# Attention and experts on one core: transposes with 112 columns, scores without their masked quarter, one two-bank PSUM tile

## The chip, the cores and the metric

The kernel runs on one core of one Trainium2 chip. The metric is the device time in microseconds, from the first to the last instruction of the program on that core. The times below are of repeated executions; the profile is one further execution under the hardware profiler.

## The reference

A gated linear attention with a state per head, and then a mixture of eight experts of which each token uses one:

```
B, H, S, D = 4, 8, 768, 48
for t in range(S):
    state = alpha[:, :, t, :, None] * state + einsum('bhd,bhe->bhde', k[:, :, t], v[:, :, t])
    y[:, :, t] = einsum('bhd,bhde->bhe', q[:, :, t], state)
x = y as [B * S, H * D]                     # 3072 tokens, 384 features
logits = x @ w_gate + modality_bias[modality_id]
e_idx = argmax(logits); gate_w = softmax(logits)[e_idx]
for e in range(8):                          # w1 384 x 1024, w2 1024 x 384
    mask = e_idx == e
    out[mask] = gate_w[mask] * (relu(x[mask] @ w1[e]) @ w2[e])
```

## The kernel before

**Attention.** The 768 positions of each of four batches are cut into chunks of P = 128, which makes NU = 24 chunks, NC = 6 to a batch. Heads go in NP = 4 pairs; a pair lies in 128 columns, its two heads at 0 to 47 and at 64 to 111, with fill between and behind (48 and 16 columns of which hold constants). For each chunk alpha, keys and queries are loaded as [position, pair of heads] and turned by TensorE with an identity matrix (`trans`, L242, four transposes to a tensor) into [feature, position]. ScalarE copies the turned alpha to X (L251). VectorE runs two scans over the chunk's positions, one backwards (G, L256) and one forwards (Fw, L266), and multiplies the turned keys by G (kh, L282) and the turned queries by Fw (qh, L290). After that a chunk needs matmuls only:

- `natural` (L296) turns kh back into [position, feature]; ScalarE copies it to knat (L298).
- `scores` (L308) forms, for each head, keys times queries, as [source position, query position], in 16 calls of K = 48, 64 sources and 128 queries. The first head of each pair goes to one one-bank PSUM tile and the second to another, both named sc, of a ring with two places. ScalarE copies each to SBUF (L312, scT), and GpSimd sets what lies above the diagonal to zero (L313, one mask of 128 x 512 for each tile).
- `state` (L328) multiplies the state T1 by qh, and `outputs` (L335) adds v times the masked scores, into y.
- `update` (L353) forms knat times v in kv; ScalarE copies it (L355), and GpSimd adds the old state (L357) and scales by the decay (L359), which gives the next T1.

**The order.** TensorE, VectorE and ScalarE issue in the order in which the program is written (their schedule is manual); GpSimd's and SyncE's instructions are placed by the framework's scheduler, which also works out all waits between engines. The loop `for s in range(NU)` is a software pipeline: step s turns and scans chunk s, scales chunk s - 1 (`scale`) and forms its scores and its update, finishes the outputs of chunk s - 2, and writes the rows of chunk s - 3 (`rows`, L366) to memory, from where tokens are gathered later. Routing (gate logits L378, choice of the expert, places in lists) is done in pieces between these, and small products of it use the PSUM name sc too. The order of TensorE in a step is: the transposes, `natural`, `logits`, `state(s - 2)`, `scores(s - 1)`, `outputs(s - 2)`, `update(s - 1)`.

**Experts.** Tokens of an expert are gathered (GpSimd's indirect DMA, xg, L689; their gate weights gg, L695), turned (L970) and split into a high and a low part (xH, xL), as are the weights (w1H, w1L, w2H, w2L). Each product is three matmuls. A slot's first layer (L1016 to L1018) writes to tiles tr; ScalarE and VectorE apply relu and split (hH L824, hL L826). The second layer takes the slot in units of 128 tokens: `layer2` makes 24 matmuls of 128x384 for a unit (L997 to L999), all into one PSUM tile op, taken as a place of the ring sc, and then `store` lets ScalarE scale it by the gate weights into SBUF (os, L1031), from where GpSimd's DMA scatters it to the output (L963). The slots come in this order: E0 and E1 with two units each (tokens known early), S1, S2 and S3 with four, S4 with four and, between its units, the steps of `short` (the short slot H of at most 32 tokens: L1055, L1067, L1074, beginning with transposes into a place of sc), S5 with four. The last unit of all is stored in another tile (of).

PSUM has the ring sc (two places of one bank), the ring tr (three), kv, and y.

## Time and profile before

| | us |
|---|---|
| median of 3 runs | 372.45 |
| lowest, highest | 371.29, 372.73 |
| the profiled execution, its time | 370.39 |
| its span in the profile | 368.4 |
| busy: TensorE | 356.4 (97%) |
| busy: VectorE | 219.1 (59%) |
| busy: ScalarE | 189.5 (51%) |
| busy: GpSimd | 154.5 (42%) |

About 2.0 us of the profiled execution lie around the span. Engines are named PE (TensorE's matmuls), PEld (its weight loads), DVE (VectorE), ACT (ScalarE), POOL (GpSimd) and SP (SyncE). In the time line a row gives the start, the duration, the engine, the line of the kernel, the operation, the tile written and those read, and the count of instructions run together in the row; behind it stands, in square brackets, how long the engine was idle before and what ended that. Rows of groups give, behind the bar, busy time, mean duration in ns, and the idle time of the engine ahead of them with what ended it. The mean granted clock of TensorE is 0.996. fp32 matmuls appear in the trace as two records to each call, transposes as one.

### The profile page before, as it was taken

To read this page: it belongs to the slowest core of one execution; us is meant where nothing else is said; L and a number is where in the kernel's file an instruction comes from. 1 tells how busy PE (TensorE), PEld (TensorE's weight loads), DVE (VectorE), ACT (ScalarE), POOL (GpSimd) and SP (SyncE) were. 2 spreads that over 40 slices of the span, in tenths; PEclk is the share of its full clock that TensorE was granted. 3 is DMA by queue.
4 is the path that set the end of the run, shared out by engine and by line. 5 is a ranking of instruction groups with operands and counts; after the bars stand their busy time and mean duration, and the time that the engine had idled before them with its cause. 6 is when DMAs were issued, how large, how long until landed. Compare 5 with 4: busy or idle time off the path is not lost. (4 is left out here: it accounts for less than half of the span.)

```text
span 368.4 us, 9336 instructions
## 1 busy us (share of the span) xinstructions
PE 356.4 (97%) x3666; PEld 315.6 (86%) x3666; DVE 219.1 (59%) x420; ACT 189.5 (51%) x367; POOL 154.5 (42%) x236
## 2 busy tenths in 40 slices
PE   8899999999999999999899999999999999999993
PEld 4689888889888887899788998899889988978992
DVE  6877979777979985888555415522660456036400
ACT  2766777777767764347454325524551554154310
POOL 9845346435436663047247326313712471220021
PEclk9999999999999999999999999999999999999998
DMA  9999999999999994887756317332733473110011
GB/s 135 166 161 178 187 190 206 195 181 189 200 198 184 213 347 165 292 323 240 246 149 220 107 62 254 111 107 83 240 93 122 133 226 134 44 44 5 1 45 50
DMA packets 122730, 59.18 MB, mean 161 GB/s; under 512 B 102857, under 2 KB 114168, under 8 KB 122676
## 3 DMA queue, kind: packets, MB, share of 16 engines
q1 hardware_dynamic: 118196, 48.78, 58.8%
q0 software_dynamic: 4032, 9.68, 7.7%
q8 instruction: 31, 0.51, 0.6%
q14 instruction: 23, 0.19, 0.2%
q10 hardware_dynamic: 448, 0.01, 0.1%
HBM read 49.01 MB, written 9.50 MB: 159 GB/s over the span
## 5 line engine op out<-in xcount | busy, mean ns | idle before, releaser
L963 POOL DMA_INDIRECT out_dram<-os,odx x23 | 23.5, 1023 | 102.9 <-ACT os L1031 93.2
L997 PE MATMUL sc<-w2H,hH 128*128 128x384 f32 x192 | 65.1, 339 | 0.0
L999 PE MATMUL sc<-w2H,hL 128*128 128x384 f32 x192 | 64.2, 334 | 0.0
L998 PE MATMUL sc<-w2L,hH 128*128 128x384 f32 x192 | 64.2, 334 | 0.0
L834 DVE TENSOR_TENSOR w1L<-w1r,w1H 128x768 fp32r<-128x768 f32 x24 | 22.0, 956 | 65.6 <-ACT w1H L832 65.6
L1016 PE MATMUL tr<-xH,w1H 128*128 128x512 f32 (+1 forms) x144 | 53.8, 374 | 0.0
L1018 PE MATMUL tr<-xH,w1L 128*128 128x512 f32 (+1 forms) x144 | 53.5, 372 | 0.0
L1017 PE MATMUL tr<-xL,w1H 128*128 128x512 f32 (+1 forms) x144 | 53.5, 371 | 0.0
L826 DVE SCALAR_TENSOR_TENSOR hL<-tr,hH 128x512 fp32r<-128x512 f32 x47 | 32.4, 689 | 30.6 <-ACT hH L824 30.6
L824 ACT ACTIVATE hH<-tr 128x512 fp32r<-128x512 f32 x47 | 28.1, 598 | 43.1 <-PE tr L1018 41.7
L1031 ACT ACTIVATE os<-sc,gg 128x384 f32<-128x384 f32 x23 | 13.4, 582 | 66.9 <-PE sc L999 40.7
L313 POOL TENSOR_SCALAR_AFFINE_SELECT scT<-scT 128x512 f32<-128x512 f32 x48 | 38.7, 830 | 21.6 <-ACT scT L312 21.5
L695 POOL DMA_INDIRECT gg<-gd,idx x25 | 27.0, 1079 | 27.5 <-DMA gd<-gs 20.5
L997 PEld LDWEIGHTS sc<-w2H,hH 128*128 128x128 f32 x192 | 36.1, 188 | 1.1 <-issue 1.0
L998 PEld LDWEIGHTS sc<-w2L,hH 128*128 128x128 f32 x192 | 36.1, 188 | 0.1
L999 PEld LDWEIGHTS sc<-w2H,hL 128*128 128x128 f32 x192 | 36.0, 188 | 0.0
L266 DVE TENSOR_TENSOR_SCAN Fw<-X,DF 128x516 f32<-128x516 f32 x24 | 32.4, 1351 | 0.8
L312 ACT COPY scT<-sc 128x512 f32<-128x512 f32 x48 | 25.8, 590 | 11.9 <-PE sc L308 11.5
L689 POOL DMA_INDIRECT xg<-xd,idx x25 | 26.5, 1059 | 11.5 <-issue 4.9
L1018 PEld LDWEIGHTS tr<-xH,w1L 128*128 128x128 f32 x144 | 27.1, 188 | 4.7
L1017 PEld LDWEIGHTS tr<-xL,w1H 128*128 128x128 f32 x144 | 27.1, 188 | 4.6
L1016 PEld LDWEIGHTS tr<-xH,w1H 128*128 128x128 f32 x144 | 27.1, 188 | 4.6
(244 smaller groups left out, 674.2 us busy)
## 6 DMA issues: line engine op xcount, KB each, us to landing
w1r<-in_moe_w_dram SPq DMA_DIRECT2D x16, 768.0 KB, 4.7
w2r<-in_moe_w_dram SPq DMA_DIRECT2D x16, 768.0 KB, 5.6
nat_a<-in_alpha_dram SPq DMA_DIRECT2D x24, 192.0 KB, 5.0
nat_k<-in_k_dram SPq DMA_DIRECT2D x24, 192.0 KB, 5.3
nat_q<-in_q_dram SPq DMA_DIRECT2D x24, 192.0 KB, 4.4
vt<-in_v_dram SPq DMA_DIRECT2D x24, 192.0 KB, 4.8
xd<-xs SPq DMA_DIRECT2D x24, 192.0 KB, 5.3
xg<-xd,idx POOLq DMA_INDIRECT x25, 5.0
```

Of the source, the lines that this page charges most:

```text
L266: vec.tensor_tensor_scan(Fw, x[:, :-1], d, 0.0, op0=ALU.mult, op1=ALU.add)
L313: pool.affine_select(s, s, [[0, NP], [1, P]], ALU.is_ge, 0.0, base=0, channel_multiplier=-1)
L689: pool.indirect_dma_start(xg[x][:, u], None, xd[0:rows], IOA(idx[:, c : c + 1], 0), bounds_check=rows - 1, oob_is_err=False)
L695: pool.indirect_dma_start(gg[x][:, u : u + 1], None, gd[0:rows], IOA(idx[:, c : c + 1], 0), bounds_check=rows - 1, oob_is_err=False)
L824: act.activation(hH, hp, AF.Relu)
L826: vec.scalar_tensor_tensor(hL, hp, 0.0, hH.bitcast(F32), op0=ALU.max, op1=ALU.subtract)
L997: pe.matmul(op, hH[:, us] if f is None else hH[:, f, us], wH, start=first, stop=False)
L998: pe.matmul(op, hH[:, us] if f is None else hH[:, f, us], wL, start=False, stop=False)
L999: pe.matmul(op, hL[:, us] if f is None else hL[:, f, us], wH, start=False, stop=final)
L1016: pe.matmul(hp, wH[:, d, fs], XH[:, d, :n], start=(d == 0), stop=False)
L1017: pe.matmul(hp, wH[:, d, fs], XL[:, d, :n], start=False, stop=False)
L1018: pe.matmul(hp, wL[:, d, fs], XH[:, d, :n], start=False, stop=(d == ND - 1))
```

## The change

**112 columns.** W = 64 + D = 112. `trans` turns the first 112 columns of each pair only, and everything in [feature, position] (X, DF, G, Fw, kh, qh, T1, S, kv, amin) has 112 partitions instead of 128. `natural` turns 112 partitions back to 112 columns, and the second head of a pair is multiplied with 48 rows or columns instead of 64 in `state` and `update`.

**Scores.** The quarter of each head's 128 x 128 scores in which sources 64 to 127 meet queries 0 to 63 is masked as a whole, and is no longer computed. Both tiles are one tile of two banks with a single place; eight calls are 128 queries wide and eight 64. In heads 4 to 7 the two halves of the sources are swapped: `scale_keys` writes kh for them in that order (two multiplications of 256 elements instead of one of 512), and v is loaded in three pieces (one for heads 0 to 3, and one for each half of heads 4 to 7). ScalarE makes three copies instead of two, one of 128 partitions x 512 elements and two of 64 partitions x 256, into one of two fixed tiles ST whose masked quarters are set to zero once at the start (four memsets). GpSimd's two masks are 64 partitions x 512 elements each, one for the blocks of the diagonal on either half. `outputs` reads the blocks of heads 4 to 7 with their order reversed (`turned`).

**PSUM.** All small users of sc have one place (bufs=1). From the experts on, OP is one tile of two banks, and `layer2` writes `OP[:, c % 2]`, so units take turns in its banks. The transposes of `short` go to tr. Paths that run in unlikely cases only (`whole`, `part`) take a one-bank tile.

Below is what TensorE has in layer 2 of slot S1, at the seam from the first unit to the second, before the change (L997 to L999; the numbers behind the names tell tiles apart, and the tile written stands ahead of the arrow):

```order
L999 MATMUL sc_3680<-w2H_3645,hL_3629 128x384
L997 MATMUL sc_3680<-w2H_3645,hH_3641 128x384
L998 MATMUL sc_3680<-w2L_3647,hH_3641 128x384
L999 MATMUL sc_3680<-w2H_3645,hL_3643 128x384
L997 MATMUL sc_3710<-w2H_3549,hH_3531 128x384
L998 MATMUL sc_3710<-w2L_3551,hH_3531 128x384
L999 MATMUL sc_3710<-w2H_3549,hL_3533 128x384
```

The second unit writes another tile, sc_3710, and has no wait of its own; of the four units of S1, the third and the fourth have one for ScalarE. After the change the same place reads (L1031 to L1033 are the same three matmuls):

```order
L1033 MATMUL sc_3142<-w2H_3673,hL_3657 128x384
L1031 MATMUL sc_3142<-w2H_3673,hH_3669 128x384
L1032 MATMUL sc_3142<-w2L_3675,hH_3669 128x384
L1033 MATMUL sc_3142<-w2H_3673,hL_3671 128x384
L1031 MATMUL sc_3142<-w2H_3577,hH_3559 128x384 [waits Activation_49]
L1032 MATMUL sc_3142<-w2L_3579,hH_3559 128x384
L1033 MATMUL sc_3142<-w2H_3577,hL_3561 128x384
```

Both units write the one tile sc_3142, and the first matmul of the second unit has a wait for ScalarE. So have those of the third and the fourth.

In the attention loop, TensorE's scores, outputs and update of one step stand before the change as follows (vt and knat belong to v and the turned keys):

```order
L308 MATMUL sc<-qh,kh 64x128 [waits DVE_49]
L308 MATMUL sc<-qh,kh 64x128 x15
L335 MATMUL y<-scT,vt_109 64x128 [waits Pool_49]
L335 MATMUL y<-scT,vt_109 64x128
L335 MATMUL y<-scT,vt_109 64x128 [waits Pool_49]
L335 MATMUL y<-scT,vt_109 64x128 x5
L353 MATMUL kv<-vt_111,knat 64x48 [waits DMAHW3_49,DVE_49,Activation_49]
L353 MATMUL kv<-vt_111,knat 64x48 x7
```

After the change they are these:

```order
L332 MATMUL sc<-qh,kh 64x128 [waits DVE_49]
L332 MATMUL sc<-qh,kh 64x128 x3
L332 MATMUL sc<-qh,kh 64x64 x4
L332 MATMUL sc<-qh,kh 64x128 x4
L332 MATMUL sc<-qh,kh 64x64 x4
L367 MATMUL y<-scT_104,vt_107 64x128 [waits Pool_49]
L367 MATMUL y<-scT_104,vt_107 64x128 x7
L385 MATMUL kv<-vt_109,knat 64x48 [waits DMAHW1_49,DVE_49,Activation_49]
L385 MATMUL kv<-vt_109,knat 48x48
L385 MATMUL kv<-vt_109,knat 64x48
L385 MATMUL kv<-vt_109,knat 48x48
L385 MATMUL kv<-vt_109,knat 64x48 [waits DMAHW3_49,DMAHW2_49]
```

Half of the 16 score calls are 64 wide, the outputs wait once for GpSimd instead of twice, and the update waits a second time, for the two pieces of v of heads 4 to 7.

The diff, cut to its core (the places where only 128 partitions become W, or bufs=2 goes, are left out):

```diff
+W = 64 + D
...
+    HALF = (slice(0, 64), slice(64, P))
+    ST = [ac.tile([P, 2, 2 * NP, 64], F32, name=f"scT{i}") for i in range(2)]
+    def quarters(t):
+        return t.rearrange("p g (a c) x -> p (g a) c x", c=4)
...
-                dst = VT[i % NV][:, :, :D] if n == "v" else nat[n, i % NB][:, :, :D]
-                sp.dma_start(dst, t[b, :, c * P : (c + 1) * P, :].rearrange("h t d -> t h d"))
+                if n == "v":
+                    vt = VT[i % NV]
+                    sp.dma_start(vt[:, :4, :D], t[b, :4, c * P : (c + 1) * P, :].rearrange("h t d -> t h d"))
+                    for m in range(2):
+                        t0 = c * P + 64 * (1 - m)
+                        sp.dma_start(vt[HALF[m], 4:, :D], t[b, 4:, t0 : t0 + 64, :].rearrange("h t d -> t h d"))
...
+    for t in ST:
+        for b in range(2):
+            pool.memset(quarters(t)[HALF[1 - b], :, 3 * b], 0.0)
...
     def trans(i, n):
-        p = ps.tile([P, NP, P], F32, name="tr", bufs=3)
+        p = ps.tile([W, NP, P], F32, name="tr", bufs=3)
         for j in range(NP):
             pe.transpose(
-                p[:, j], nat[n, i % NB][:, 2 * j : 2 * j + 2].rearrange("p a b -> p (a b)"), ident
+                p[:, j], nat[n, i % NB][:, 2 * j : 2 * j + 2].rearrange("p a b -> p (a b)")[:, :W], ident
             )
...
     def scale_keys(i):
-        kh = sb.tile([P, NP, P], F32, name="kh")
+        kh = sb.tile([W, NP, P], F32, name="kh")
         pk = trans(i, "k")
-        vec.tensor_tensor(kh, pk, seg(st[i, "G"][:, 1:], 1), op=ALU.mult)
+        g = seg(st[i, "G"][:, 1:], 1)
+        vec.tensor_tensor(kh[:, :2], pk[:, :2], g[:, :2], op=ALU.mult)
+        ko, po, go = (x[:, 2:].rearrange("p a (m x) -> p a m x", m=2) for x in (kh, pk, g))
+        vec.tensor_tensor(ko[:, :, ::-1], po, go, op=ALU.mult)
...
     def natural(i):
         p = ps.tile([P, NP, P], F32, name="tr", bufs=3)
         for j in range(NP):
-            pe.transpose(p[:, j], st[i, "k"][:, j], ident)
-        kn = na.tile([P, NP, P], F32, name="knat", bufs=2)
-        act.copy(kn, p)
+            pe.transpose(p[:, j, :W], st[i, "k"][:, j], ident[:W, :W])
+        kn = na.tile([P, NP, W], F32, name="knat", bufs=2)
+        act.copy(kn, p[:, :, :W])
...
-        pp = [ps.tile([P, NP, P], F32, name="sc", bufs=2) for _ in range(2)]
-        for j in range(NP):
+        pp = ps.tile([P, 2, 2 * NP, 64], F32, name="sc")
+        for a in range(2):
             for m in range(2):
-                for g in range(2):
-                    r, z = slice(64 * g, 64 * g + D), slice(64 * m, 64 * m + 64)
-                    pe.matmul(pp[g][z, j], kh[r, j, z], qh[r, j], start=True, stop=True)
-        st[i, "s"] = []
-        for g in range(2):
-            s = sb.tile([P, NP, P], F32, name="scT", bufs=4)
-            act.copy(s, pp[g])
-            pool.affine_select(s, s, [[0, NP], [1, P]], ALU.is_ge, 0.0, base=0, channel_multiplier=-1)
-            st[i, "s"].append(s)
+                for b in range(2):
+                    for g in range(2):
+                        j, z = a + 2 * b, HALF[b ^ m]
+                        r = slice(64 * g, 64 * g + D)
+                        o = pp[z, g, 4 * a + 2 * b + m : 4 * a + 2 * b + 2]
+                        pe.matmul(o, kh[r, j, z], qh[r, j, 64 * m :], start=True, stop=True)
+        s = ST[i % 2]
+        sv, pv = quarters(s), quarters(pp)
+        act.copy(sv[:, :, 1:3], pv[:, :, 1::2])
+        for b in range(2):
+            act.copy(sv[HALF[b], :, 3 * b], pv[HALF[b], :, 2 * b])
+        for m in range(2):
+            e = s.rearrange("p g (j m) x -> p (g j) m x", m=2)[HALF[m], :, m]
+            pool.affine_select(e, e, [[0, 2 * NP], [1, 64]], ALU.is_ge, 0.0, base=0, channel_multiplier=-1)
+        st[i, "s"] = s
...
+    def turned(s, g, j):
+        b, a = divmod(j, 2)
+        t = s[:, g, 4 * a + 2 * b : 4 * a + 2 * b + 2]
+        return t[:, ::-1] if b else t
...
-                sc[g][:, j],
+                turned(sc, g, j),
...
-        kv = ps.tile([P, NP, D], F32, name="kv")
+        kv = ps.tile([W, NP, D], F32, name="kv")
         for h in range(H):
-            r = slice(64 * (h % 2), 64 * (h % 2) + 64)
+            r = slice(64 * (h % 2), min(64 * (h % 2) + 64, W))
             pe.matmul(kv[r, h // 2], kn[:, h // 2, r], vt[:, h, :D], start=True, stop=True)
...
+    OP = ps.tile([P, 2, T], F32, name="sc")
...
-    def layer2(h, w2, x, u, c, per, keep=False):
+    def layer2(h, w2, x, u, c, per, keep=False, banks=True):
         us = slice(u * P, (u + 1) * P)
-        op = ps.tile([P, DM], F32, name="sc", bufs=2)
+        op = OP[:, c % 2, :DM] if banks else ps.tile([P, DM], F32, name="sc")
...
     def short(x, w, c):
-        xp = ps.tile([P, ND, P], F32, name="sc", bufs=2)
+        xp = ps.tile([P, ND, P], F32, name="tr", bufs=3)
```

More of the change, by code (lines that the diff above doesn't have):

```diff
@@ L132, in load @@
             if n in names:
-                dst = VT[i % NV][:, :, :D] if n == "v" else nat[n, i % NB][:, :, :D]
-                sp.dma_start(dst, t[b, :, c * P : (c + 1) * P, :].rearrange("h t d -> t h d"))
+                if n == "v":
[4 more added lines that the diff above has]
+                        sp.dma_start(vt[HALF[m], 4:, :D], t[b, 4:, t0 : t0 + 64, :].rearrange("h t d -> t h d"))
+                else:
+                    sp.dma_start(
+                        nat[n, i % NB][:, :, :D], t[b, :, c * P : (c + 1) * P, :].rearrange("h t d -> t h d")
+                    )
     wgs = cp.tile([P, ND, E], F32, name="wgs")
@@ L158, in attention_moe @@
             )
-    DR = na.tile([P, SEGS], F32, name="DR")[:, : NP * SEG + 1]
+    DR = na.tile([W, SEGS], F32, name="DR")[:, : NP * SEG + 1]
     vec.memset(DR, AFLOOR)
@@ L163, in attention_moe @@
     for i in range(2):
-        t = na.tile([P, SEGS], F32, name=f"X{i}")[:, : NP * SEG + 1]
+        t = na.tile([W, SEGS], F32, name=f"X{i}")[:, : NP * SEG + 1]
         vec.memset(t[:, 0 :: SEG], 0.0)
         X.append(t)
-        t = na.tile([P, SEGS], F32, name=f"DF{i}")[:, : NP * SEG]
+        t = na.tile([W, SEGS], F32, name=f"DF{i}")[:, : NP * SEG]
         vec.memset(t, 0.0)
@@ L170, in attention_moe @@
     for i in range(3):
-        t = ac.tile([P, NP, 64], F32, name=f"T1{i}")
+        t = ac.tile([W, NP, 64], F32, name=f"T1{i}")
         pool.memset(t[:, :, D:], 0.0)
@@ L177, in attention_moe @@
     gacc = ac.tile([P, NU], F32, name="gacc")
-    amin = ac.tile([P, NU, NP], F32, name="amin")
+    amin = ac.tile([W, NU, NP], F32, name="amin")
     junk = ac.tile([P, DM], F32, name="junk")
@@ L216, in bias_table @@
         yield
-        mp = ps.tile([P, NU], F32, name="sc", bufs=2)
+        mp = ps.tile([P, NU], F32, name="sc")
         pe.transpose(mp, mf, ident[:NU, :NU])
@@ L254, in decay @@
         x = X[i % 2]
-        G = na.tile([P, SEGS], F32, name="G", bufs=4)[:, : NP * SEG + 1]
+        G = na.tile([W, SEGS], F32, name="G", bufs=4)[:, : NP * SEG + 1]
         vec.tensor_tensor_scan(
@@ L264, in decay_back @@
         vec.reciprocal(d[:, 0::SEG], G[:, 1::SEG])
-        Fw = na.tile([P, SEGS], F32, name="Fw", bufs=3)[:, : NP * SEG]
+        Fw = na.tile([W, SEGS], F32, name="Fw", bufs=3)[:, : NP * SEG]
         vec.tensor_tensor_scan(Fw, x[:, :-1], d, 0.0, op0=ALU.mult, op1=ALU.add)
@@ L287, in scale @@
             scale_keys(i)
-        qh = sb.tile([P, NP, P], F32, name="qh", bufs=3)
+        qh = sb.tile([W, NP, P], F32, name="qh", bufs=3)
         pq = trans(i, "q")
@@ L326, in state @@
         for j, h, g, z in tiles4():
-            r = slice(64 * g, 64 * g + 64)
+            r = slice(64 * g, min(64 * g + 64, W))
             pe.matmul(
@@ L349, in update @@
         kn, vt = st[i, "n"], VT[i % NV]
-        kv = ps.tile([P, NP, D], F32, name="kv")
+        kv = ps.tile([W, NP, D], F32, name="kv")
         for h in range(H):
-            r = slice(64 * (h % 2), 64 * (h % 2) + 64)
+            r = slice(64 * (h % 2), min(64 * (h % 2) + 64, W))
             pe.matmul(kv[r, h // 2], kn[:, h // 2, r], vt[:, h, :D], start=True, stop=True)
-        S1 = sb.tile([P, NP, D], F32, name="S")
+        S1 = sb.tile([W, NP, D], F32, name="S")
         act.copy(S1, kv)
@@ L357, in update @@
             pool.tensor_tensor(S1, S1, T1[i % 3][:, :, :D], op=ALU.add)
-        A = st[i + 1, "G"][:, 1::SEG].unsqueeze(2).broadcast_to([P, NP, D])
+        A = st[i + 1, "G"][:, 1::SEG].unsqueeze(2).broadcast_to([W, NP, D])
         pool.tensor_tensor(T1[(i + 1) % 3][:, :, :D], S1, A, op=ALU.mult)
@@ L452, in route_flow @@
         yield
-        rp = ps.tile([P, n, E], F32, name="sc", bufs=2)
+        rp = ps.tile([P, n, E], F32, name="sc")
         pe.matmul(rp, tri, oh[:, s], start=True, stop=False)
@@ L534, in route_early @@
         yield
-        cnt = ps.tile([P, E], F32, name="sc", bufs=2)
+        cnt = ps.tile([P, E], F32, name="sc")
         pe.matmul(cnt, ones, ohs, start=True, stop=(s == 0))
@@ L565, in route_early @@
         yield
-        tp = ps.tile([P, 2], F32, name="sc", bufs=2)
+        tp = ps.tile([P, 2], F32, name="sc")
         for t in range(n):
@@ L699, in attention_moe @@
     fl = cp.tile([P, 2], F32, name="fl")
+    pool.memset(fl, 1.0)
     flb = cp.tile([P, 1], BF16, name="flb")
@@ L704, in out_of_range @@
         vec.tensor_reduce(fl[:, 0:1], gacc, axis=AX.X, op=ALU.max)
[L705 removed]
+        vec.tensor_reduce(fl[:W, 1:2], amin.rearrange("p a b -> p (a b)"), axis=AX.X, op=ALU.min)
         vec.tensor_scalar(fl[:, 0:1], fl[:, 0:1], 0.0, None, op0=ALU.is_gt)
@@ L709, in out_of_range @@
         yield
-        fp = ps.tile([P, 1], F32, name="sc", bufs=2)
+        fp = ps.tile([P, 1], F32, name="sc")
         pe.matmul(fp, ones, flb, start=True, stop=True)
@@ L1172, in whole @@
         for u, c in enumerate(slot_cols(s)):
-            layer2(h, w2p, 0, u, c, 1)
+            layer2(h, w2p, 0, u, c, 1, banks=False)
     def part(s, us):
@@ L1182, in part @@
             w2p = [split2(0, j) for j in range(4)]
-            op = ps.tile([P, DM], F32, name="sc", bufs=2)
+            op = ps.tile([P, DM], F32, name="sc")
             for f in range(NF):
```

1 line of the change is left out of this document (removed).

## The prediction

> **What bounds the kernel now.** First the page's busy times, then the busy time by stretch (start and end of the stretch, its length, and the busy time of each engine in it).
>
> ```profile
> PE 356.4 (97%) x3666; PEld 315.6 (86%) x3666; DVE 219.1 (59%) x420; ACT 189.5 (51%) x367; POOL 154.5 (42%) x236
> ```
>
> ```profile
> 20.00:140.00 120.00, 120.00 (x2208) 105.15 (x2207) 100.54 (x198) 86.44 (x197) 59.76 (x99) 1.00 1.05 202
> ...
> 240.00:368.00 128.00, 122.16 (x668) 110.70 (x666) 45.01 (x57) 46.51 (x74) 35.65 (x35) 0.99 0.30 95
> ```
>
> TensorE is busy 120.00 of 120.00 us in the attention stretch and 122.16 of 128.00 in the last experts, and what is missing there lies behind the last matmul, while the final store drains. So whatever takes TensorE longer, or makes it wait, in either stretch comes out whole at the end, and whatever takes it less is gained whole, unless another engine becomes late. Next the time line of TensorE in one attention step, in which the scores are L308, the state update L353 and the transposes L242 and L296.
>
> ```profile
> 60.34 1.06 PE L308 MATMUL sc<-qh,kh 48*64 48x128 f32 x32
> 61.32 1.09 PE L335 MATMUL y<-scT,vt 128*64 128x128 f32 x16
> 62.25 0.62 PE L353 MATMUL kv<-vt,knat 128*64 128x48 f32 x16
> 62.80 0.66 PE L242 MATMUL tr<-ident,nat_a 128*128 128x128 f32 x4
> 63.29 0.60 PE L242 MATMUL tr<-ident,nat_k 128*128 128x128 f32 x4
> 63.73 0.60 PE L242 MATMUL tr<-ident,nat_q 128*128 128x128 f32 x4
> ...
> 64.85 0.60 PE L296 MATMUL tr<-ident,kh 128*128 128x128 f32 x4
> 65.38 0.67 PE L328 MATMUL y<-qh,T 64*64 64x128 f32 x16
> ```
>
> Durations are modelled and overlap, so I use distances between starts. The scores take 61.32 - 60.34 = 0.98 us, the update 62.80 - 62.25 = 0.55, four transposes 63.73 - 63.29 = 0.44. Last, the seam between two units of layer 2, with the row that groups the stores to SBUF (each reads one unit's result out of PSUM, scaled).
>
> ```profile
> 243.25 0.33 PE L999 MATMUL sc<-w2H,hL 128*128 128x384 f32 x1
> ...
> 243.42 0.33 PE L997 MATMUL sc<-w2H,hH 128*128 128x384 f32 x1
> ...
> 243.67 0.58 ACT L1031 ACTIVATE os<-sc,gg 128x384 f32<-128x384 f32 x1 [2.80 <-issue]
> ```
>
> ```profile
> L1031 ACT ACTIVATE os<-sc,gg 128x384 f32<-128x384 f32 x23 | 13.4, 582 | 66.9 <-PE sc L999 40.7 <-issue 23.8 <-DMA gg<-gd,idx 2.3
> ```
>
> TensorE goes from the last matmul of a unit to the first of the next in 0.17 us, the pace inside a unit, and the store runs beside the next unit's matmuls. That overlap costs nothing now.
>
> **Layer 2: a wait at the seam.** Before, the units of a slot take turns in two PSUM tiles, and only the third and fourth wait, for a store two units back. After, they all write one two-bank tile, in alternate banks; and the order shows the first matmul of the second unit with a wait for ScalarE that it did not have. It cannot be for hH or the weights, which the first unit has waited for already; the only newer ScalarE work is the store of the first unit. So each unit waits for the store directly before it, although that reads the other bank. Its price, by the rows above: the store starts 0.42 us after the last matmul's start and takes 0.58, and the release costs about what it costs in the other direction (the last matmul ends at 243.25 + 0.33 = 243.58, the store starts at 243.67: 0.09). The next unit starts 0.42 + 0.58 + 0.09 = 1.09 us after that last matmul instead of 0.17: 0.92 us. Behind the waiting matmul stands all of TensorE's work, and no later wait takes it back: TensorE has none in this stretch but the short ones at xg.
>
> E1 has one plain seam, and S1, S2, S3 and S5 three each: 13 x 0.92 = 12.0 us. In S4 the short slot's work lies between the units:
>
> ```profile
> 312.57 0.58 ACT L1031 ACTIVATE os<-sc,gg 128x384 f32<-128x384 f32 x1 [2.99 <-issue]
> ```
>
> ```profile
> 313.85 0.44 PE L997 MATMUL sc<-w2H,hH 128*128 128x384 f32 x1
> ...
> 318.28 0.43 PE L997 MATMUL sc<-w2H,hH 128*128 128x384 f32 x1
> ```
>
> ```profile
> 318.39 0.58 ACT L1031 ACTIVATE os<-sc,gg 128x384 f32<-128x384 f32 x1 [4.02 <-PE sc L999]
> ...
> 322.78 0.58 ACT L1031 ACTIVATE os<-sc,gg 128x384 f32<-128x384 f32 x1 [3.55 <-issue]
> ...
> 324.05 0.44 PE L997 MATMUL sc<-w2H,hH 128*128 128x384 f32 x1
> ```
>
> The first and third store there end (313.15, 323.36) before the next unit starts (313.85, 324.05): nothing. The middle one ends at 318.97, so the unit at 318.28 slips to 319.06: 0.8 us. E0 is the odd one, since its first store waits for gates that are still being gathered:
>
> ```profile
> 162.46 0.43 PE L997 MATMUL sc<-w2H,hH 128*128 128x384 f32 x1
> ...
> 165.59 0.58 ACT L1031 ACTIVATE os<-sc,gg 128x384 f32<-128x384 f32 x1 [1.64 <-DMA gg<-gd,idx]
> ```
>
> ```profile
> 168.25 1.02 POOL L689 DMA_INDIRECT xg<-xd,idx  x1 [0.78 <-DVE vals L525]
> ```
>
> ```profile
> 175.58 0.38 PE L970 MATMUL kv<-ident,xg 128*128 128x128 f32 x2
> 177.44 0.33 PE L970 MATMUL kv<-ident,xg 128*128 128x128 f32 x1 [1.48 <-DMA xg<-xd,idx]
> 177.94 0.33 PE L970 MATMUL kv<-ident,xg 128*128 128x128 f32 x1 [0.17 <-DMA xg<-xd,idx]
> ```
>
> The second unit, at 162.46 now, would have to wait until 165.59 + 0.58 + 0.09 = 166.26: 3.8 us. Part is given back: TensorE waits for gathered tokens later (1.48 + 0.17, and about 0.25 of slow filling between: 1.9), and that gather hangs on VectorE's vals, computed from matmuls ahead of 162.46, so it does not move. 3.8 - 1.9 = 1.9, with 3.8 as the bound if the gather does move. Layer 2 together: 12.0 + 0.8 + 1.9 = **14.7 us**. The moved transposes of the short slot (from sc to tr) I cost at nothing.
>
> **Scores.** Sixteen calls of 128 columns become eight of 128 and eight of 64. They go in groups of four tiles, 8 groups in 0.98 us: 0.122 each. By width alone a half group costs 0.061. The nearest row, the update with 48 columns, makes 8 groups of two in 0.55, 0.069 each, changeover included; with that as floor the step gains 4 x (0.122 - 0.069) = 0.21. If what costs is not the width but the number of calls (16 records in 0.55 against 32 in 0.98 is the same per record), it gains nothing. The narrow groups have the scores' own shape, so I stay near the upper end, less something for the swapped order of the tiles, which no row prices: 0.16 a step, in 22 steps where TensorE is full: **-3.5 us**, bounds 0 and -5.4.
>
> **What follows the scores.** The first copy, ScalarE's, was all that the first mask needed; now it needs a copy of 128x512 and one of 64 partitions by 256. ScalarE, then GpSimd, in the step above, and the end of a later step:
>
> ```profile
> 60.48 0.36 ACT L380 COPY lts<-kv 128x256 f32<-128x256 f32 x1
> 61.50 1.08 ACT L312 COPY scT<-sc 128x512 f32<-128x512 f32 x2 [0.66 <-PE sc L308]
> ```
>
> ```profile
> 62.16 2.15 POOL L313 TENSOR_SCALAR_AFFINE_SELECT scT<-scT 128x512 f32<-128x512 f32 x2 [1.44 <-ACT scT L312]
> 64.28 0.59 POOL L357 TENSOR_TENSOR S<-S,T 128x192 f32<-128x192 f32 x1
> 64.94 0.52 POOL L359 TENSOR_TENSOR T<-S,G 128x192 f32<-128x192 f32 x1
> ```
>
> ```profile
> 102.89 0.52 POOL L359 TENSOR_TENSOR T<-S,G 128x192 f32<-128x192 f32 x1
> ```
>
> ```profile
> 104.00 0.32 PE L328 MATMUL y<-qh,T 64*64 64x128 f32 x1
> ```
>
> Two copies start 1.08 - 0.59 = 0.49 apart, so the mask starts 0.49 + 0.36 - 0.59 = 0.26 us later after the scores. The masks keep their size (512 elements each) and stand ahead of the T chain on GpSimd. At 65.46 the chain ends as L328 starts (65.38): no slack; at 103.41 it has 0.59. I count four steps of the first kind: 4 x 0.26 = **+1.0**; with all 20 it were 5.2. Keys are scaled in two halves instead of one 0.69 us instruction:
>
> ```profile
> 63.93 0.69 DVE L282 TENSOR_TENSOR kh<-tr,G 128x512 f32<-128x512 f32 x1
> ```
>
> ```profile
> 163.25 0.42 DVE L990 TENSOR_TENSOR xL<-y,xH 128x256 fp32r<-128x256 f32 x1 [0.44 <-ACT xH L989]
> ```
>
> 2 x 0.42 - 0.69 = 0.15 at most, for L296 and for VectorE's next scan; it shows in the few steps where kh comes last, say **+0.3** in all, bound 22 x 0.15 = 3.3. At the start, v in three transfers instead of one and four more memsets on GpSimd: **+0.2**, bound 1.
>
> **112 columns.** The transposes keep 128 moving columns, with 112 weight columns in place of 128. Two rows price that: a transpose with only 20 weight columns (L678), and what follows it.
>
> ```profile
> 155.12 0.27 PE L678 MATMUL kv<-ident,gt 128*20 128x128 f32 x1
> 155.23 0.17 PE L711 MATMUL sc<-flb,ones 128*128 128x1 bf16 x1
> ```
>
> With a sixth of the columns it holds TensorE 0.11 us, as one of the four does (0.44 / 4). So the width of the weights does not set the pace, and I count nothing. Only L296 moves 112 columns now: at most an eighth of 0.44 in 20 steps, 1.1, which I leave to the range. [...]
>
> Operands of 112 partitions instead of 128 keep their elements per partition; a store of 32 partitions takes what one of 128 does (582 ns above):
>
> ```profile
> L1087 ACT ACTIVATE os<-tr,gg 32x384 f32<-32x384 f32 x1 | 0.6, 572 | 0.0
> ```
>
> So they count for nothing. **Sum:** attention -3.5 + 1.0 + 0.3 + 0.2 = -2.0; layer 2 +14.7; together +12.7. The profiled execution had 370.39, so 383.1; the median of the runs lies 2.06 above it, at 372.45: **385.1, say 385**. Bounds that I take in: layer 2 from 13.5 (release free) to 17, attention -4.5 to +2: 381.5 to 391.5.
>
> **The rivals.** (1) *The other side: the banks are kept apart.* The wait in the order stands for something already done, so the seams cost nothing; it decides whether the second unit's first matmul starts before or after the store's end. Then only attention counts: 372.45 - 2.0 = 370.5, or 368 with the whole gain. For it: the units do write different banks. Against it: a wait that is in the program is waited for, and I know nothing else that explains this one. [...] 0.07. (2) *Attention loses.* GpSimd's chain becomes late in every step, 5.2 instead of 1.0, or the scores gain nothing: 4 us more, 389. Against it are the 0.59 us at 103; for it, VectorE's 100.54 of 120 us and two masks that take 2.15 us in the step above. 0.14. (3) *Narrower transposes pay after all,* a load-bound TensorE: 288 x (0.11 x 16/128) = 4.0 less, 381. Against it the 20-column row. 0.05. (4) *The change's saving isn't there in E0's seam:* the gather moves along, 1.9 more, 387. 0.10. My forecast has the other 0.64.
>
> **How the numbers follow.** 381 to 390 holds forecast, (2), (3) and (4) but for their edges; (1) and those edges are left out. A measurement of this kernel can tell about 0.5%, 1.9 us, from no change. All but (1) are slower by more: slower 0.92; of (1), 0.06 faster and the rest, with a part of the edges, the same, 0.02.
>
> **What would show it.** In the profile after: stores of layer 2 followed by the next unit's first matmul, about 1.1 us after the last one's start in 13 seams, idle time on PE of that line put down to ScalarE's store, 3.8 us in E0 and shorter waits at xg; the scores in about 0.8 us; transposes at 0.44 as now. If the first matmul of a second unit starts before the preceding store ends, the largest term is wrong, and so is the sign. If TensorE idles in attention ahead of L355 of the new listing, rival (2) holds.

## The result, and the profile after

| | us |
|---|---|
| after, median of 4 runs | 396.18 (395.51 to 398.85) |
| before, median of 4 runs on the same chip | 372.59 (371.29 to 375.14) |
| ratio, with its 95% interval | 1.0636 [1.0593, 1.0678] |
| the profiled execution after, its time; its span | 395.84; 394.1 |
| forecast | 385.0 (381 to 390) |

The kernel is slower by 23.6 us, where 12.7 were forecast. The page's row of busy times, and the group with the idle time that grew most:

```profile
PE 360.6 (91%) x3666; PEld 315.8 (80%) x3666; DVE 222.3 (56%) x444; ACT 192.3 (49%) x391; POOL 158.5 (40%) x241
...
L1031 PE MATMUL sc<-w2H,hH 128*128 128x384 f32 x192 | 67.5, 352 | 13.7 <-ACT os L1065 13.7
```

TensorE is 4.2 us busier, with less to compute, and has 91% of a longer span instead of 97%: it waits, and it is slower at times. The waits of TensorE, first from 30 to 150 us (attention; before the change, nothing is listed there at all), then from 150 us on (us in total, times, the longest):

```profile
PE tr L260 <- DMA nat_a<-in_alpha_dram: 5.0, 6, 2.4
PE sc L332 <- DVE rk L493: 1.5, 1, 1.5
PE sc L332 <- issue: 0.7, 2, 0.4
...
PE sc L1031 <- ACT os L1065: 13.7, 15, 4.0
```

The last row is the forecast's seam. The first was not forecast: TensorE waits six times for alpha to be loaded. In the time line of TensorE and ScalarE these are, in this order, the longest wait for alpha, a shorter one behind the scores, the last scores, the seam of E0 and the seam of E1:

```profile
47.96 0.65 PE L260 MATMUL tr<-ident,nat_a 128*112 128x128 f32 x4 [2.40 <-DMA nat_a<-in_alpha_dram]
...
48.88 1.05 PE L260 MATMUL tr<-ident,nat_q 128*112 128x128 f32 x4
49.73 1.06 PE L398 MATMUL tr<-ident,yt 128*128 128x128 f32 x4
...
74.42 0.85 PE L332 MATMUL sc<-qh,kh 48*64 48x128 f32 x32
75.20 1.09 PE L367 MATMUL y<-scT,vt 128*64 128x128 f32 x16
77.72 0.62 PE L260 MATMUL tr<-ident,nat_a 128*112 128x128 f32 x4 [1.43 <-DMA nat_a<-in_alpha_dram]
78.18 0.60 PE L260 MATMUL tr<-ident,nat_k 128*112 128x128 f32 x4
78.61 0.60 PE L260 MATMUL tr<-ident,nat_q 128*112 128x128 f32 x4
...
145.12 0.90 PE L332 MATMUL sc<-qh,kh 48*64 48x128 f32 x32 [1.53 <-DVE rk L493]
...
174.24 0.69 PE L1031 MATMUL sc<-w2H,hH 128*128 128x384 f32 x1 [4.00 <-ACT os L1065]
174.72 0.53 PE L1032 MATMUL sc<-w2L,hH 128*128 128x384 f32 x1
175.04 0.53 PE L1033 MATMUL sc<-w2H,hL 128*128 128x384 f32 x1
...
194.55 0.34 PE L1033 MATMUL sc<-w2H,hL 128*128 128x384 f32 x1
194.92 0.58 ACT L1065 ACTIVATE os<-sc,gg 128x384 f32<-128x384 f32 x1 [2.76 <-PE sc L1033]
195.56 0.44 PE L1031 MATMUL sc<-w2H,hH 128*128 128x384 f32 x1 [0.67 <-ACT os L1065]
195.83 0.33 PE L1032 MATMUL sc<-w2L,hH 128*128 128x384 f32 x1
```

Four things are to be read here. The scores take 75.20 - 74.42 = 0.78 us instead of 0.98, and four transposes still 78.61 - 78.18 = 0.43. Behind the wait of 2.40 us the transposes take 0.85 (48.88 to 49.73), twice their time. Behind the 4.00 us at E0 the matmuls follow each other at 0.32 instead of 0.17. And at a plain seam the next unit starts 195.56 - 194.55 = 1.01 us after the last matmul instead of 0.17, and its second matmul 0.27 after the first instead of 0.17. Why things took twice as long shows in the busy time by stretch, with the granted clock third from the end:

```profile
48.00:50.00 2.00, 2.00 (x14) 2.00 (x15) 0.78 (x3) 0.59 (x1) 0.00 (x0) 0.72 0.42 74
50.00:52.00 2.00, 2.00 (x16) 1.39 (x14) 1.97 (x3) 0.91 (x2) 0.13 (x1) 0.50 1.18 213
52.00:54.00 2.00, 2.00 (x54) 1.52 (x48) 1.25 (x2) 1.53 (x6) 0.06 (x1) 0.93 1.15 230
...
78.00:80.00 2.00, 2.00 (x21) 1.92 (x19) 1.19 (x3) 0.88 (x2) 0.00 (x0) 1.00 0.92 214
...
176.00:178.00 2.00, 2.00 (x8) 2.00 (x8) 1.23 (x11) 0.00 (x0) 1.43 (x2) 0.50 0.75 158
178.00:180.00 2.00, 2.00 (x12) 2.00 (x11) 0.00 (x0) 0.00 (x0) 1.62 (x2) 0.85 1.00 388
```

The clock falls to a half around the two long waits, at 48.9 us and, while TensorE still waits, at 171.8 us. It comes back 3.4 and 6.8 us later. After the wait of 1.43 us (78 to 80) it does not fall.

**Where the 25 us of the profile went.** The start of TensorE's last matmul moves from 361.82 to 386.99, by 25.2. The start of the last chunk's scores moves from 137.8 to 145.1 (7.4 of it), the first unit of E0 by 0.2 more: attention, 7.6, forecast -2.0. E0 costs 4.0: its second unit starts 4.2 later (4.00 of them waiting), half clock adds 2.0, and 2.2 is given back at xg, where TensorE no longer waits; forecast 1.9. The 13 plain seams cost 0.96 to 1.00 each (from the first matmul of layer 2 in S1 to that in S2, with three seams between, 37.21 us instead of 34.32, and from S2 to S3 37.26 instead of 34.28), together 12.8, forecast 12.0; the one in S4 costs 0.8, as forecast. 7.6 + 4.0 + 12.8 + 0.8 = 25.2.

### The profile page after: what moved, and what is told of

The parts are those of the page before. It is cut to its first block, busy times and chain, and to the rows that moved or that the text cites. A ratio compares the mean times of both kernels' runs of the same rounds, so it can differ in the third digit from the quotient of the medians.

```text
span 394.1 us, 9523 instructions
## 1 busy us (share of the span) xinstructions
PE 360.6 (91%) x3666; PEld 315.8 (80%) x3666; DVE 222.3 (56%) x444; ACT 192.3 (49%) x391; POOL 158.5 (40%) x241
## 5 line engine op out<-in xcount | busy, mean ns | idle before, releaser
L1031 PE MATMUL sc<-w2H,hH 128*128 128x384 f32 x192 | 67.5, 352 | 13.7 <-ACT os L1065 13.7
L997 POOL DMA_INDIRECT out_dram<-os,odx x23 | 23.1, 1004 | 116.8 <-ACT os L1065 107.8
L1033 PE MATMUL sc<-w2H,hL 128*128 128x384 f32 x192 | 65.1, 339 | 0.0
L1032 PE MATMUL sc<-w2L,hH 128*128 128x384 f32 x192 | 65.0, 339 | 0.0
L1031 PEld LDWEIGHTS sc<-w2H,hH 128*128 128x128 f32 x192 | 36.7, 191 | 19.3 <-ACT os L1065 18.8
L340 POOL TENSOR_SCALAR_AFFINE_SELECT scT<-scT 64x512 f32<-64x512 f32 x48 | 39.5, 823 | 25.9 <-ACT scT L337 20.6
L1033 PEld LDWEIGHTS sc<-w2H,hL 128*128 128x128 f32 x192 | 36.6, 191 | 0.0
L284 DVE TENSOR_TENSOR_SCAN Fw<-X,DF 112x516 f32<-112x516 f32 x24 | 33.0, 1376 | 0.8
L274 DVE TENSOR_TENSOR_SCAN G<-X,DR 112x516 f32<-112x516 f32 x24 | 31.0, 1294 | 0.0
```

The costliest lines, as they stand in the source:

```text
L274: vec.tensor_tensor_scan(G[:, 1:][:, ::-1], x[:, 1:][:, ::-1], DR[:, 1:][:, ::-1], 0.0, op0=ALU.mult, op1=ALU.max)
L284: vec.tensor_tensor_scan(Fw, x[:, :-1], d, 0.0, op0=ALU.mult, op1=ALU.add)
L340: pool.affine_select(e, e, [[0, 2 * NP], [1, 64]], ALU.is_ge, 0.0, base=0, channel_multiplier=-1)
L1031: pe.matmul(op, hH[:, us] if f is None else hH[:, f, us], wH, start=first, stop=False)
L1032: pe.matmul(op, hH[:, us] if f is None else hH[:, f, us], wL, start=False, stop=False)
L1033: pe.matmul(op, hL[:, us] if f is None else hL[:, f, us], wH, start=False, stop=final)
```

## The experiments

The theory at first: the seams are the wait on one tile, and what attention loses comes from v in three transfers. Rivals for attention: the single place of the ring sc, or the copies and masks behind the scores. "Step" below is the time from the scores of one chunk to those of the next.

### Layer 2 in one tile or two

e1 gives the changed kernel two one-bank tiles in the experts; the attention loop is as it was.

```diff
+    SC = [sctx.enter_context(tc.tile_pool(name="psc", bufs=1, space=PSUM))]
...
-    OP = ps.tile([P, 2, T], F32, name="sc")
+    sctx.close()
+    SC[0] = ctx.enter_context(tc.tile_pool(name="pso", bufs=2, space=PSUM))
...
-        op = OP[:, c % 2, :DM] if banks else ps.tile([P, DM], F32, name="sc")
+        op = SC[0].tile([P, DM], F32, name="sc")
```

> The changed kernel, but with layer 2's units taking turns in two one-bank PSUM tiles (as before) in place of the two banks of one. Theory (the wait on one tile is what layer 2 lost): 13 seams x 0.98, 0.8 in S4 and 4.0 around E0 go, 17.6 us, so about 378.5 us; what stays above the kernel before, about 6, is the attention stretch. Rival (the seams are slow for another reason, the two-bank place or the stores): still 393 or more.

e2 is the opposite: the kernel before, with layer 2 alone in one two-bank tile (and the transposes of the short slot in tr, as in the change).

```diff
-        op = ps.tile([P, DM], F32, name="sc", bufs=2)
+        op = OP[:, c % 2, :DM] if banks else SC[0].tile([P, DM], F32, name="sc")
```

> The kernel before, with nothing changed but layer 2: all units write the banks of one two-bank tile in turn (and the short slot's transposes go to tr). Theory: the whole loss of layer 2 and nothing else, 372.5 + 17.6 = 390 us. Rival (the loss needs the rest of the change): under 380.

e1 had 377.74 us, 1.0114 [1.0067, 1.016] of before, 18.4 less than the whole change; e2 had 388.37, 1.0399 [1.0351, 1.0447], 15.6 more than before. TensorE's waits in e1 (attention) and, below, in e2 (experts):

```profile
PE tr L262 <- DMA nat_a<-in_alpha_dram: 7.1, 9, 2.4
```

```profile
PE sc L1002 <- ACT os L1036: 13.2, 15, 3.5
```

In e1 no wait for the store is left, and alpha is as late as ever; in e2 the 15 waits appear in a kernel that has nothing else of the change. E0 waits 3.47 us there, and in the stretch from 168 to 172 us the clock is 0.50 again. So the tile, and nothing else, makes the seams: the units write different banks, and the wait is one for the tile.

### v in one transfer or three

e3 is the changed kernel with v loaded at once (heads 4 to 7 then meet their v unswapped, so their output differs). e4 is the kernel before with v in three pieces, shaped as in the change but in natural order, and e4c has three pieces that all span 128 partitions, by heads 0 to 3, 4 to 5, 6 to 7.

```diff
-                    sp.dma_start(vt[:, :4, :D], t[b, :4, c * P : (c + 1) * P, :].rearrange("h t d -> t h d"))
-                    for m in range(2):
-                        t0 = c * P + 64 * (1 - m)
-                        sp.dma_start(vt[HALF[m], 4:, :D], t[b, 4:, t0 : t0 + 64, :].rearrange("h t d -> t h d"))
+                    sp.dma_start(vt[:, :, :D], t[b, :, c * P : (c + 1) * P, :].rearrange("h t d -> t h d"))
```

> The changed kernel with v loaded in one transfer per chunk instead of three; heads 4 to 7 then meet v in unswapped order, so that part of the product is another one, of the same size. Theory (seven transfers to a step instead of five make alpha late, because each waits for the eighth before it): the waits for alpha go (5.0 us) and with them the half clock after the longest of them (about 1.7) and the lead at the start: 390 us. Rival (the scores' longer copies, masks and halved key scaling delay attention): 395 or more.

> The kernel before with v loaded in the three pieces of the change (heads 0 to 3, and 64 positions each of heads 4 to 7, in unswapped order), and nothing else. Theory (number of transfers): waits for alpha in attention and 3 to 7 us more, 376 to 379 us. Rival (the loads are harmless, the lateness of alpha follows from the scheduler's order in the changed kernel): 372.5.

> The kernel before with v in three transfers again, but cut by heads (0 to 3, 4 and 5, 6 and 7), all of 128 partitions. Theory (the number of transfers counts, seven to a step with eight in flight): as with the three pieces before, 376 to 379 us, with a wait for alpha of 2 us or more and half clock behind it. Rival (it is the two pieces of 64 partitions that are slow): 372.5.

| | us | ratio to before | waits for alpha, 30 to 150 us |
|---|---|---|---|
| e3, change with v at once | 388.82 | 1.0422 [1.0375, 1.047] | 0.2 |
| e4, before with three pieces | 377.51 | 1.0124 [1.0081, 1.0167] | 2.7, one wait |
| e4c, three pieces by heads | 377.87 | 1.0132 [1.0089, 1.0175] | 2.1, one wait |

The two late alphas in the time line of TensorE, e4 and then e4c:

```profile
42.37 1.08 PE L249 MATMUL tr<-ident,nat_a 128*128 128x128 f32 x4 [2.71 <-DMA nat_a<-in_alpha_dram]
```

```profile
42.00 0.85 PE L248 MATMUL tr<-ident,nat_a 128*128 128x128 f32 x4 [2.11 <-DMA nat_a<-in_alpha_dram]
```

So the pieces cost 7.4 us in the changed kernel (396.18 - 388.82) and 4.8 in the kernel before (377.51 against 372.76 of before). Their shape makes no difference to the time: three by heads (377.87) cost as much as three by halves (377.51). The step with the wait takes 10.56 us in e4 instead of 5.1, more than the 2.71 waited; the clock is at 0.50 from 42 to 48 us.

### The place in PSUM, and the 112 columns alone

e5 is the kernel before with the scores in one two-bank tile and a single place for it and for routing's small products; e6 is the changed kernel with these small products in the ring tr; e8 (112) is the kernel before with the 112 columns only.

```diff
-        pp = [ps.tile([P, NP, P], F32, name="sc", bufs=2) for _ in range(2)]
+        p2 = SC[0].tile([P, 2, NP, P], F32, name="sc")
+        pp = [p2[:, g] for g in range(2)]
```

> The kernel before with both score tiles as one tile of two banks with one place, and the small routing products in that one place too (layer 2 keeps two tiles). Theory (in the last step the scores must wait until VectorE has read a routing product from the same place): a wait of about 1.5 us ahead of the scores of the last chunk, 373.5 to 375 us. Rival (that wait belongs to the masks or the halved keys): 372.5.

```diff
-        rp = ps.tile([P, n, E], F32, name="sc")
+        rp = ps.tile([P, n, E], F32, name="tr", bufs=3)
```

> The changed kernel with the small routing products in the ring tr instead of in the scores' one place. Theory: the wait of the scores for rk (1.5 us) and that of L568 for the copies (0.4) go, nothing else: 394 to 395 us. Rival (those waits only hide what VectorE is late with anyway): 396.

> The kernel before with 112 columns and partitions in place of 128 throughout attention, and nothing else of the change. Theory (the width of the weights doesn't set the pace of a transpose): 371.5 to 373, the transposes at 0.44 us per four. Rival (they do, by 16/128): 368.5 us.

e5 had 372.93 us, 0.9996 [0.9972, 1.0021]: one place alone costs nothing, and the expectation that put the late steps down to it missed. e6 had 394.05, 1.0568 [1.0529, 1.0606], 2.1 less than the changed kernel. Its waits in attention:

```profile
PE tr L260 <- DMA nat_a<-in_alpha_dram: 4.5, 6, 1.9
PE tr L317 <- ACT xs L402: 0.9, 3, 0.3
```

The 1.5 us for rk are gone, and small waits in tr have come. The single place cost time only where VectorE was late with a small product: 1.5 us for rk in the changed kernel, ahead of the last chunk's scores, and no wait for rk is listed in e5.

The 112 columns alone had 370.27, 0.9942 [0.9917, 0.9968]: a small gain. In the time line, an attention step (compare 64.85 to 65.38 before):

```profile
62.56 0.60 PE L243 MATMUL tr<-ident,nat_k 128*112 128x128 f32 x4
63.00 0.60 PE L243 MATMUL tr<-ident,nat_q 128*112 128x128 f32 x4
...
64.11 0.55 PE L297 MATMUL tr<-ident,kh 112*128 112x112 f32 x4
64.59 0.67 PE L329 MATMUL y<-qh,T 64*64 64x128 f32 x16
```

Transposes with 112 weight columns still take 0.44; those that move 112 columns (L297) take 0.48 instead of 0.53, and the steps are 0.01 to 0.08 us shorter.

### Whose time the pieces take

The kernel before issues five transfers a chunk on SyncE (alpha, keys, queries, v, and the rows xd), the changed one seven. My first reading was that too many were in flight at once: each transfer waits in the program for one eight places ahead of it. By the trace that one had landed 0.8 us or more earlier each time in the changed kernel (from 14 to 135 us), and the reading fell. What the time line of SyncE shows between two alphas of the changed kernel (duration: of the row; the trace puts 66.2 us of waits for PE and ACT down to SyncE from 20 to 140 us before, and 46.6 in the changed kernel, and these may lie inside the rows):

```profile
34.66 0.38 SPq L147 DMA_DIRECT2D nat_a<-in_alpha_dram  x1
35.13 1.66 SPq L147 DMA_DIRECT2D nat_k<-in_k_dram  x1
...
37.48 0.82 SPq L142 DMA_DIRECT2D vt<-in_v_dram  x1
38.34 1.27 SPq L145 DMA_DIRECT2D vt<-in_v_dram  x2
...
43.59 0.57 SPq L147 DMA_DIRECT2D nat_a<-in_alpha_dram  x1
```

SyncE's rows follow each other with 0.04 to 0.12 us between them here, and 0.52 once, ahead of 48.63. Two small pieces of v take it 1.27 us, 0.63 each for 48 KB, where a whole alpha of 192 KB takes 0.4 to 0.6 here and keys of the same size once 1.66. From one alpha's issue at 27.84 to another's at 50.35 stand 28 issues whose durations add up to 19.8 of the 22.5 us. But the rows of the kernel before, with five transfers, follow each other at 0.09 us too:

```profile
39.86 0.39 SPq L134 DMA_DIRECT2D nat_a<-in_alpha_dram  x1
40.34 0.79 SPq L134 DMA_DIRECT2D vt<-in_v_dram  x1
41.23 1.40 SPq L134 DMA_DIRECT2D nat_k<-in_k_dram  x1
42.73 0.74 SPq L134 DMA_DIRECT2D nat_q<-in_q_dram  x1
43.56 1.94 SPq L371 DMA_DIRECT2D xd<-xs  x1
45.59 0.39 SPq L134 DMA_DIRECT2D nat_a<-in_alpha_dram  x1
```

So a full track doesn't tell the two kernels apart, and neither does the mean time of an issue: with gaps it is 0.80 us in the 22.5 us above and about 1.1 here (15 issues from 28.69 to 45.59). Fewer transfers take longer each; what the waits in the rows have of that was not tried. What tells them apart is SyncE's pace, from the 11th alpha's issue to the 21st's: 5.25 us a chunk before (49.96 to 102.50) and 5.62 in the changed kernel (56.21 to 112.39). From the transposes of one chunk to those of the next, TensorE takes 5.53 there before, and 5.41 in the changed kernel with v at once (e3). Five transfers thus leave SyncE 0.28 us of a step to spare, two more take 0.37, and SyncE becomes the slower of the two. Nor are the data the limit: the DMA engines' share from 20 to 140 us is 1.05 before and 0.92 in the changed kernel. Two theories: (a) the order, which the scheduler chooses on SyncE, puts too much ahead of alpha; (b) SyncE has no time for seven. The experiments below tell them apart, and (b) from the data behind the pieces. First, another engine issues the two small pieces, in the kernel before: ScalarE (e8, scalar; `act` for `pool` in the line below) and GpSimd (e9).

```diff
-                        sp.dma_start(vt[64 * m : 64 * m + 64, 4:, :D], t[b, 4:, t0 : t0 + 64, :].rearrange("h t d -> t h d"))
+                        pool.dma_start(vt[64 * m : 64 * m + 64, 4:, :D], t[b, 4:, t0 : t0 + 64, :].rearrange("h t d -> t h d"))
```

> The kernel before with v in the three pieces, of which ScalarE issues the two small ones. ScalarE's transfers share the eight places of SyncE's by the order, so: theory (eight in flight, over both queues): the wait for alpha around 45 us stays, 376 us or more. Rival (SyncE's own time to issue a transfer is what is short): no wait for alpha, 372.5 to 374, with ScalarE about 1.3 us a step busier.

> The kernel before with v in the three pieces, of which GpSimd issues the two small ones; its transfers have places of their own. Theory and rival both: no wait for alpha around 45 us. If GpSimd's two issues a step (about 1 us each by its gathers) make the state late, waits for T or the masks appear instead and the time is 374 to 378; if not, 372.5 to 373.5.

ScalarE had 398.35, 1.07 [1.0644, 1.0756], and its waits tell that the experiment missed its aim:

```profile
PE tr L303 <- ACT X L258: 7.0, 2, 6.8
```

ScalarE's own copies stood behind its transfers; what SyncE gained can't be seen. GpSimd had 373.69, 1.0033 [0.9998, 1.0068], and no wait for alpha was left from 30 us on. Its busy time by stretch (GpSimd's is the last with a count):

```profile
20.00:140.00 120.00, 119.18 (x2146) 104.33 (x2146) 100.28 (x190) 84.69 (x193) 96.37 (x142) 1.00 1.10 200
```

GpSimd pays, with 96.37 us busy instead of 59.76, but it had the time. The same data in the same pieces then cost nothing clear of noise, and what moved was who issues them, and with it whose eight places they take.

Then, the order: e11 is the changed kernel with two tiles in layer 2 (as e1) and SyncE held to the order of the program, e12 the kernel before with three pieces and that order, e13 the kernel before with that order alone, e14 with that order and the 112 columns.

```diff
-    mctx.enter_context(tc.manual_schedule(engines=manual))
+    mctx.enter_context(tc.manual_schedule(engines=manual | {mybir.EngineType.SP}))
```

> The whole change (it computes the reference), with layer 2 in two tiles and SyncE's loads in the loop in the order of the program (alpha of the chunk three ahead first, then keys, queries and v of the chunk two ahead, then the rows) instead of the scheduler's. If it is the order (a): no waits for alpha above 0.5 us, 370 to 372 us. If it is SyncE's issue time (b): waits for alpha of 2 us or more remain, 375 to 379.

> The kernel before with v in three transfers (377.5 us with the scheduler's order), SyncE's loads in the order of the program. (a): 372 to 373.5 us, no wait of 2 us for alpha. (b): 376 to 378.

> The kernel before with SyncE's loads in the order of the program, nothing else. Both theories: 372 to 373, since alpha is not late before; this is what the two runs above are held against.

> The kernel before with 112 columns (370.3 us so far) and SyncE's loads in the order of the program; computes the reference. Both theories: 370 to 371 us.

| | us | ratio to before |
|---|---|---|
| e11, change, two tiles, program order | 376.99 | 1.0182 [1.013, 1.0233] |
| e12, before, three pieces, program order | 378.77 | 1.0206 [1.0154, 1.0259] |
| e13, before, program order | 370.41 | 0.9978 [0.9948, 1.0009] |
| e14, before, 112 columns, program order | 369.44 | 0.9955 [0.9922, 0.9988] |

The waits of e11 and of e12 in attention:

```profile
PE tr L262 <- DMA nat_q<-in_q_dram: 5.1, 6, 1.5
```

```profile
PE tr L249 <- DMA nat_q<-in_q_dram: 4.5, 7, 1.3
```

With the order put right alpha is in time and the queries are late instead, by as much or more in total: (a) falls. The waits of 2 us or more for alpha, expected of (b), did not come either, since the loss is now in six or seven shorter waits for the queries. With five transfers (e13) the order costs nothing, and TensorE has no wait there.

Last, whether it is the issue or what the pieces carry: e15 is the kernel before with v at once and two loads of 192 bytes a chunk into tiles that nothing reads; e16 has v in two halves, six transfers a chunk.

```diff
+                if n == "v":
+                    for m in range(2):
+                        sp.dma_start(XT[2 * (i % NV) + m], t[b, m : m + 1, c * P, :])
```

> The kernel before with two more loads a chunk on SyncE, each of 48 numbers (192 bytes) of v into a scratch tile that nothing reads; v itself stays one transfer. If SyncE's time to issue is what the pieces of v cost, whatever they carry: a tiny load takes it about 0.6 us too, alpha or queries come late once or more by 2 us or over, and the time is about that of v in three pieces, 376 to 378.5. If it is what lies behind SyncE (the descriptors and the data of the pieces): one descriptor each weighs nothing, no wait over 0.5 us on a load in attention, and 372 to 373.5.

> The kernel before with v in two transfers, heads 0 to 3 and heads 4 to 7, six transfers a chunk instead of five or seven. If it is the sum of the issues against the length of a step: at the mean of 0.80 us an issue six take 4.8 us of a step of 5.04 to 6.4, so SyncE just keeps up: 372 to 374, at most one wait of about 1 us on a load. If each transfer more costs about the same: half of what three pieces cost, 375, with waits of 1 to 2 us.

e15 had 377.37, 1.0127 [1.0075, 1.0179], what three pieces of v have; e16 had 373.51, 1.0015 [0.998, 1.0051]. The wait in e15, and SyncE's time line ahead of it:

```profile
PE tr L246 <- DMA nat_a<-in_alpha_dram: 2.2, 1, 2.2
```

```profile
37.00 0.39 SPq L135 DMA_DIRECT2D nat_a<-in_alpha_dram  x1
37.67 1.40 SPq L138 DMA_DIRECT2D xt<-in_v_dram  x5
39.17 0.39 SPq L135 DMA_DIRECT2D vt<-in_v_dram  x1
39.61 1.30 SPq L138 DMA_DIRECT2D xt<-in_v_dram  x4
...
44.14 1.09 SPq L135 DMA_DIRECT2D nat_a<-in_alpha_dram  x1
```

Loads that carry next to nothing make alpha late as well, while the DMA engines' share is 0.61 from 34 to 48 us instead of 1.07 before. They take 0.23 to 0.42 us each instead of 0.63, but the scheduler has bunched them (26 between 28 and 47 us), so e15 shows that issues alone are enough, not that two tiny ones a chunk would do in every order; that its time is that of three pieces is chance. In this bunch the wait for the transfer eight places ahead does bind now and then: the gap of 0.28 us ahead of 37.67 ends as that one lands. Six transfers (e16) just go: SyncE's pace is 5.29 us a chunk, and there are two waits for alpha, 0.7 us in all. The expectation for e16 had 4.8 us for six issues, which was too low; that the time came out as expected is in part luck. e15 shows that the number of transfers counts, as it adds only loads of one row of 192 bytes; larger transfers than those of before were not tried.

### Everything together

e7 is the changed kernel with two tiles and v at once (heads 4 to 7 unswapped, so their output differs); e10 is the whole change with two tiles, the small pieces issued by GpSimd.

> The changed kernel with both repairs: layer 2 in two tiles, and v in one transfer (so heads 4 to 7 meet v in unswapped order, another product of the same size). Theory (the two causes are separate and hold nearly the whole loss): 396.2 - 18.4 - 7.4 = 370.4 us, below the kernel before. Rival (they overlap, or the scores' longer chain costs by itself): 374 or more.

> The whole change, with layer 2 in two tiles and the two small pieces of v issued by GpSimd; it computes the reference. If the loads are repaired that way: 370 to 371.5 us, faster than the kernel before. If GpSimd's chain (masks, then the state) gets late: 374 to 378.

e7 had 371.42, 0.9952 [0.9924, 0.998]. By e1 and e3, 396.18 - 18.4 - 7.4 = 370.4 was due, so the two causes add up, and hold all but the last 1 us of the loss. e10 had 376.74, 1.0132 [1.0066, 1.0198], with waits for what GpSimd does:

```profile
PE y L369 <- POOL scT L342: 2.1, 4, 1.2
```

The remedy that served the kernel before (e9) comes out no better here than the pieces left on SyncE (e1, 1.0114): TensorE now waits for the masks, which share GpSimd with the transfers. The whole change with six transfers a chunk was not tried. What is faster than before in these runs, and computes all that it computes, is the part with 112 columns: e8 (112) and e14, each about 0.5%; of e14's gain about half is in e13 too, which has the order alone.

## Why the prediction was wrong

**The step that failed** is "At the start, v in three transfers instead of one and four more memsets on GpSimd: +0.2, bound 1". It looked for the cost at the start only, and took the pieces for data that is hidden. They are issues, and SyncE makes them in every chunk: with seven its pace is 5.62 us, more than the 5.41 that TensorE needs for a step (e3), so it falls behind until an input is late. Shown by e3 (-7.4 us), e4 (+4.8), e9 (another engine, no loss), e11 and e12 (another order, the same wait elsewhere), e15 (issues with next to no data, a late alpha) and e16 (six, no loss). Why two more issues lengthen SyncE's chunk by 0.37 us, and not by the 1.27 that they take themselves, stays open. No row of the prediction had SyncE in it: before, its time line already has rows on 15.5 of 16.9 us, from one alpha at 28.69 to another at 45.59.

**What was missing beside it** is the clock. A wait was priced at its own length. TensorE's clock went to half around the waits of 2.40 and 4.00 us, which cost about 1.4 us more at 48 us (the step took 9.18 instead of 5.34 in e3, 3.8 longer, with 2.4 of waiting) and 2.0 more at E0. The first of these is in part chance: in e1 TensorE waits 2.40 us for alpha too, ahead of 49.09 us, and the clock stays at 1.00 from 46 to 54 us.

**Layer 2: right.** The wait for the store directly before, its 13 places and the one in S4 came out as worked, 0.98 a seam against 0.92. E0's wait was 4.0 for 3.8, and what xg gave back 2.2 for 1.9; the half clock made E0 4.0 us instead of 1.9. Layer 2 had 17.6 for 14.7, just over its bound of 17, and e1 and e2 bear the mechanism out from both sides. Rival (1), banks kept apart, fell with it, and so did rival (4), since the gather did not move along. Whether the chip by itself needs a wait between two banks was not shown, since the program has the wait in every kernel with one tile.

**Scores: right, and smaller than what came with them.** 0.20 us a step of gain for 0.16 forecast. From the scores of the 4th chunk to those of the 21st e3 takes 91.5 us and before 93.8 (by the starts of the scores): 2.3 less in 17 steps, 0.14 a step, with the copies, the keys in halves and the shorter transposes back in it. The masks' chain on GpSimd, the core of rival (2), is not what attention lost: e7, which has it, has no loss. But the last three steps of e3 take 2.8 us longer than before's: waits for a mask (1.3), kh (0.5) and a copy (0.4), and the two stops named at the end.

**112 columns: the transposes right, L296 too low.** They stay at 0.44, and rival (3) falls. The weight loads themselves do get shorter with 112 columns, 144 to 137 ns for the keys (mean, before and after), but the pace of the transposes does not follow. The gain of 0.58% [0.32, 0.83], about 2.2 us, is more than the 1.1 left to the range, for which L297 accounts for 1.0; the rest is in shorter steps whose cause was not tried.

**Why the range missed it.** It took attention from -4.5 to +2, and attention had +7.6. A term with a bound of 1 us cost 7.4, and so was outside by more than six.

## What to carry to other kernels

Before splitting a transfer, see in the time line of the issuing engine how much of a step it has left: here 0.28 us (5.25 of 5.53), and two transfers more used it up, though their data were small. Adding up the durations is not enough, since they were longer where there were fewer of them (with gaps about 1.1 us with five, 0.80 with seven). A load of 192 bytes took 0.23 us or more on SyncE (e15), and one of 192 KB 0.37 or more (before). A tile is what is waited for here, not the bank: a ring of two tiles (e1, no wait for the store) and two halves of one tile (e2, 13.2 us of waits) are different programs. Waits of 1.52 to 4.00 us on TensorE came with a half clock of 3.4 or 6.8 us in some cases and without in others (2.40 in e1), so such a wait is to be priced with and without.

## What the runs showed of the hardware

- TensorE's clock was granted at a half behind or during idle times of 1.52 (e5, at 179 us), 1.59 (e16), 1.64 (e13), 1.71 (after, at 10.9 us), 1.91 (e6), 2.11 (e4c), 2.40 (after), 2.71 (e4), 3.47 (e2) and 4.00 us (after), for 3.4 or 6.8 us, and not after idle times of 1.43 and 1.53 in the changed kernel, 1.60 (e12), 1.87 (e4c, at 183 us) and 2.40 (e1). The mean clock of the profiled execution is 0.990 in e5, 0.989 in e16 and e13, and 0.995 in e12. So between 1.5 and 2.4 us the length of the idle time did not decide it; what did was not tried.
- In most of these profiles the scores stop twice at about 133 us for 0.3 to 0.5 us each, ended by "issue", and that step takes some 1.5 us longer (7.09 instead of 5.52 in e2 and e4). It is in the profiles of after, e1 to e5, e4c, e7, e8 (112), e10, e15 and e16, and not in those of before, e6, e8 (scalar) and e11 to e14; e9 has one such stop. So 1.4 of the 7.6 us in the profile after may not belong to the change. What it is was not tried, and it stays open.
